# Where the first keys are loaded: one of four opening loads of an attention and feed-forward kernel moves from a hardware queue to the software queue

## The chip, the cores and the metric

The kernel runs on one core of a Trainium2 chip. The core has five engines that run their own instruction streams and meet through semaphores: TensorE (PE) multiplies matrices, VectorE (DVE) and ScalarE (ACT) work on tiles, GpSimd (POOL) does the same and also issues DMAs whose descriptors it writes in software, and SyncE (SP) issues DMAs. DMAs issued from SP and ACT go through hardware queues. In this kernel all DMAs that change the type on the way, from f32 in memory to bf16 in the core, are issued from POOL. All DMAs share the core's 16 DMA engines. The metric is the device time of one execution in microseconds, median over several runs.

## The reference

The inputs q, k and v have the shape 8 x 8 x 576 x 64 (batches, heads, tokens, width of a head), all f32. Each token attends to itself and the 63 tokens before it in its batch. The result, as 4608 rows of 512, goes through a gated feed-forward block of width 1536:

```python
scores = scale * np.matmul(q, k.transpose(0, 1, 3, 2))
rel = pos[:, None] - pos[None, :]
scores = np.where((rel >= 0) & (rel < 64), scores, -1e9)
attn = softmax(scores)                      # with max and sum along the last axis
x = (attn @ v).transpose(0, 2, 1, 3).reshape(4608, 512)
g = x @ w_gate
out = (g / (1 + exp(-g)) * (x @ w_val)) @ w_out
```

## The kernel before

The 4608 tokens are cut into 36 tiles of 128 and 9 blocks of 512. Of a tile the kernel needs q and k transposed (a head's width on the partitions), from which it makes scores, exponentials, and their product with v; the result is normalised and transposed to `xT`. Of a block it makes the gate and value products with the weights `Wg` and `Wv` (12 groups of 128 columns each, four matmuls a group), the activation, and the product with `Wo`. Matmuls of the feed-forward block are most of TensorE's time. The order of the work on each engine is written out by hand in `build`: `_Graph` keeps one list of operations, gives each engine its operations in that order, and derives the semaphore waits from the keys that an operation reads and writes.

This study is about the head of the program, the first four tiles (tokens 0 to 255 are the first pair, 256 to 511 the second), which must go through attention before the feed-forward matmuls of block 0 can start:

- `loads` puts out, in this order: `first_loads`; `init` (DVE memsets, and two selects on POOL that make the triangle `tri` and the identity `ident`); `init_mask` and `init_nmask` (DVE operations that make the masks from `tri`); some memsets; then POOL's queue: `load2(1)` (q and k of the second pair, tiles `ks` and `qs`, gated on the mask `nmask`), four loads of v (`va`), the first weights (`W(0, 2)`: Wg and Wv of column groups 0 and 1), a copy of v to shifted rows (`shift`), and more weights and shifts.
- `first_loads` (L830) loads q and k of the first pair, as f32, into a part of a buffer that is still free (`hT`). Each is split into the even and the odd heads, so there are four loads of 256 KB: k even on SP, k odd on ACT, then q even on SP and q odd on ACT. A partition holds eight tokens of one head, 2 KB in one piece.
- `first_cast` (L840) turns these rows to bf16, in the buffer `ost`: k even on DVE, k odd on ACT, q even on DVE, and q odd in two parts, five of eight tokens on DVE and three on ACT.
- `first_T` (L848) transposes on TensorE. For the first pair a transpose takes 128 columns (a token's even and odd head side by side), eight for each of k and q. For the second pair, whose rows hold the even heads first and then the odd ones, it takes 64 columns, sixteen for each.
- `first_ev` copies the transposed rows out of PSUM to `kT` and `qT`.
- `warm(5)` puts five dummy f32 matmuls on a tile of zeros ahead of everything on TensorE.

On TensorE the order of the head is: the dummies, k's transposes, q's transposes, four matmuls that put the mask bias into PSUM, scores of tile 0, the second pair's transposes between further bias matmuls and scores, the products with v, the transposes to `xT`, and from then on the gate and value matmuls of block 0 (L918).

Of the kernel before, what the change touches and what calls it, by code (L numbers as in the profile page):

```python
# [17 lines left out]
BF = dt.bfloat16  # L18
# [135 lines left out]
class _Kernel:  # L154
# [18 lines left out]
    def alloc(self):  # L173
        nc = self.nc

        def sb(name, n, dtype=BF):
            return nc.alloc_sbuf_tensor(name, [128, n], dtype)

        def ring(name, cnt, n, dtype=BF):
            return [sb("%s%d" % (name, i), n, dtype) for i in range(cnt)]  # L180

        self.ident = sb("ident", 128)
        self.tri = sb("tri", 128)
        self.mask = sb("mask", 3 * 128)
        self.nmask = sb("nmask", 3 * 128)
        self.kmask = sb("kmask", 128)
        self.Wg = sb("Wg", NK * DFF)[:, :].rearrange("p (c f) -> p c f", c=NK)
        self.Wv = sb("Wv", NK * DFF)[:, :].rearrange("p (c f) -> p c f", c=NK)
        self.Wo = sb("Wo", NF * DM)[:, :].rearrange("p (c m) -> p c m", c=NF)
        self.qn = ring("qn", self.NQ, DM)  # L190
        self.kn = ring("kn", self.NQ, DM)
        self.rows = {x: ring(x + "s", 2, 2 * DM) for x in "qk"}
        self.va = [t[:, :].rearrange("p (h d) -> p h d", h=H) for t in ring("va", self.NV, H * 80)]
        self.vs = [t[:, :].rearrange("p (h d) -> p h d", h=H) for t in ring("vs", 4, H * 80)]
        self.kT = sb("kT", 4 * self.NZ * 128)[:, :].rearrange("p (c t) -> p c t", c=4)
        self.qT = sb("qT", 4 * (self.ZQ * 128 + 64))[:, :].rearrange("p (c t) -> p c t", c=4)
        self.wz = sb("wz", 512)
        self.pt = [t[:, :].rearrange("p (h x) -> p h x", h=H) for t in ring("pt", self.NP, H * 128)]
        self.rc = ring("rc", 2, 8, F32)
        self.xb = ring("xb", 4, DM)  # L200
        xT = ring("xT", self.NX, NK * 512)
        self.xT = [t[:, :].rearrange("p (c t) -> p c t", c=NK) for t in xT]
        self.sig = ring("sig", self.NS, 512)
        self.uu = ring("uu", self.NS, 512)
        hT = ring("hT", self.NH, NF * 512)
        self.hT = [t[:, :].rearrange("p (f t) -> p f t", f=NF) for t in hT]
        self.ost = ring("ost", self.NO, DM, F32)
        self.first = {}
        for i, x in enumerate("kq"):
            f = hT[1][:, 2048 * i:2048 * i + 2048].bitcast(F32).rearrange("p (e j d) -> p e j d", e=2, j=8)  # L210
            c = self.ost[i][:, :].bitcast(BF).rearrange("p (j e d) -> p j e d", j=8, e=2)
            self.first[x] = (f, [("hT", 1, 4 * i + f, j) for f in range(4) for j in range(2)], c, [("ost", i), ("osth", i)])
        self.wup = sb("wup", 1, F32)
        self.psa = nc.alloc_psum_tensor("ps", [128, 4096], F32)
        self.ps = [self.psa[:, 512 * i:512 * i + 512] for i in range(8)]
        self.rot = {"f": ([0, 1, 2, 3], 0), "a": ([4, 5, 6, 7], 0)}
        self.n_s = 0
        self.lru = False
        self.held = set()
# [610 lines left out]
        return ev  # L830

    def first_loads(self):
        for x, src in (("k", self.k), ("q", self.q)):
            f, fkeys, _, _ = self.first[x]
            for e0, eng in ((0, "sp"), (1, "act")):
                a = src[0, e0::2, 0:256, :].rearrange("c (g j) d -> g c (j d)", j=8)
                d = f[:, e0].rearrange("p j d -> p (j d)")
                self.g.op(eng, lambda e, d=d, a=a: e.dma_start(d, a), reads=fkeys, writes=[("f", x, e0)], dma=True)

    def first_cast(self, x, parts):  # L840
        f, fkeys, c, ckeys = self.first[x]
# [4 lines left out]
    def first_T(self, x, st=0):  # L846
        c, ckeys = self.lines(1, x) if st else (self.first[x][2], self.first[x][3] + self.first[x, 0])
        bank, bk = self.bank("a")  # L848
        tb = bank.bitcast(BF).rearrange("p (j t) -> p j t", j=8)

        def pe(e):
            for j in range(8):
                if st:
                    for p in range(2):
                        r = e.transpose(tb[64 * p:64 * p + 64, j, :], c[:, j, p, :], self.ident[:, :])
                else:
                    r = e.transpose(tb[:, j, :], c[:, j, :, :], self.ident[:, :])
            return r

        self.g.op("pe", pe, reads=["ident"] + ckeys, writes=[bk])  # L860
        return bank, bk
# [195 lines left out]
    def build(self):  # L1057
# [1 line left out]
        self.loads()  # L1059
        self.banks("a", [4, 5, 6, 7, 0, 1, 2, 3, 4, 5, 0, 1, 2, 3, 4, 5, 6, 7, 0, 1, 2, 3, 4, 5, 6, 7, 6, 7])  # L1060
        self.lru = True
        self.warm(5)
        self.first_cast("k", ((0, 0, 8, "dve"), (1, 0, 8, "act")))
        self.first_cast("q", ((0, 0, 8, "dve"), (1, 0, 5, "dve"), (1, 5, 8, "act")))
        fk = self.first_T("k")
        self.first_ev("k", 0, "dve", fk)
        fq = self.first_T("q")
# [208 lines left out]
```

## Time and profile before

| what | value |
|---|---|
| median of 3 runs | 325.6 us (325.49 to 325.85) |
| profiled execution, its own time | 325.72 us |
| span of the profiled execution | 324.0 us |
| TensorE matmuls, busy | 314.4 us, 97% |
| VectorE, busy | 218.6 us, 67% |
| ScalarE, busy | 125.6 us, 39% |
| GpSimd, busy | 106.5 us, 33% |
| software DMA queue | 100032 packets, 18.36 MB |
| hardware DMA queues | 48336 packets, 20.72 MB |

Rows of the timeline give the start in microseconds from the span's start, the duration, the engine, the line and the operation with its output and inputs; in square brackets stands how long the engine was idle before and what ended that. Rows of the chain give start, duration and what held the chain. "SPq", "ACTq" and "POOLq" are the sequencers that issue DMAs. An issue row ends when the descriptors are written, not when the data has landed; the last number of a DMA row tells the time from issue to landing. The KB of a DMA are those that it writes.

### The profile page before, as it was taken

How to read it: one execution, taken by the hardware profiler on the slowest of the kernel's cores; microseconds unless marked ns; L12 is line 12 of the kernel's file. 1: busy time of each engine (PE TensorE's matmuls, PEld its weight loads, DVE VectorE, ACT ScalarE, POOL GpSimd, SP SyncE). 2: the span in 40 equal slices, each digit the busy share in tenths (PEclk: the TensorE clock that was granted, in tenths of full speed). 3: DMA queues.
4: the chain of work that ended last, by engine and by line, in shares of the span. 5: the costliest groups of instructions: out<-in, count | busy, mean ns of one | idle time of the engine just before them, and what ended most of it. 6: DMA issues, size and time to landing. Idle time of an engine off the chain costs nothing.

```text
span 324.0 us, 8018 instructions
## 1 busy us (share of the span) xinstructions
PE 314.4 (97%) x3411; PEld 169.3 (52%) x3446; DVE 218.6 (67%) x408; ACT 125.6 (39%) x226; POOL 106.5 (33%) x138
## 2 busy tenths in 40 slices
PE   7989999999999999999999999999999999999996
PEld 5655677777545454545454544545454544444444
DVE  6778985788576966766767585958586767555510
ACT  3825565643433442433333232424242422222311
POOL 6999711643626061507060607060402000000000
PEclk9999999999999999999999999999999999999999
DMA  7999999999999799959997998999677212000012
GB/s 189 177 197 187 201 184 176 104 169 142 166 155 152 124 109 137 165 103 133 129 120 118 146 139 83 148 133 159 73 110 96 69 34 65 34 32 32 34 65 97
DMA packets 148403, 39.59 MB, mean 122 GB/s; under 512 B 131344, under 2 KB 143376, under 8 KB 148368
## 3 DMA queue, kind: packets, MB, share of 16 engines
q0 software_dynamic: 100032, 18.36, 71.7%
q1 hardware_dynamic: 42864, 10.89, 23.5%
q10 hardware_dynamic: 5472, 9.83, 9.5%
q8 instruction: 27, 0.44, 0.6%
q14 instruction: 8, 0.07, 0.1%
HBM read 37.75 MB, written 9.44 MB: 146 GB/s over the span
## 4 chain that ended last, share of the span: by engine, by line
PE 91%; DMA 2%; POOL 2%; issue 1%; DVE 1%; ACT 1%; ACTq 0%
PE ps L918 56%; PE ps L962 29%; DMA Wv<-in_moe_w_val_dram 2%; PE ps L729 2%; PE ps L521 2%; POOL va L325 1%; PE ps L471 1%; PE ps L475 0%; ACT xT L255 0%; PE ps L385 0%; ACT sig L899 0%; POOL ks L335 0%; PE ps L552 0%; POOL qs L335 0%; POOL Wg L345 0%
## 5 line engine op out<-in xcount | busy, mean ns | idle before, releaser
L918 PE MATMUL ps<-xT,Wv 128*128 128x512 bf16 (+1 forms) x484 | 110.4, 351 | 1.6 <-DMA Wv<-in_moe_w_val_dram 0.9
L904 DVE SCALAR_TENSOR_TENSOR uu<-sig,ps 128x512 bf16<-128x512 bf16 x108 | 73.8, 683 | 56.2 <-ACT sig L899 55.9
L918 PE MATMUL ps<-xT,Wg 128*128 128x512 bf16 (+1 forms) x481 | 107.9, 351 | 2.3 <-issue 2.2
L899 ACT ACTIVATE sig<-ps 128x512 bf16<-128x512 f32 x108 | 64.9, 603 | 89.1 <-PE ps L918 89.1
L962 PE MATMUL ps<-Wo,hT 128*128 128x512 bf16 (+1 forms) x436 | 97.4, 373 | 0.5 <-DVE hT L906 0.2
L906 DVE SCALAR_TENSOR_TENSOR hT<-uu,ps 128x512 bf16<-128x512 bf16 x108 | 74.2, 687 | 4.7 <-PE ps L918 1.0
L918 PEld LDWEIGHTS ps<-xT,Wv 128*128 128x128 bf16 x496 | 48.4, 98 | 45.7 <-DMA Wv<-in_moe_w_val_dram 1.1
L918 PEld LDWEIGHTS ps<-xT,Wg 128*128 128x128 bf16 x496 | 46.8, 98 | 42.7 <-ACT xT L255 0.2
L962 PEld LDWEIGHTS ps<-Wo,hT 128*128 128x128 bf16 x444 | 43.3, 98 | 49.0
L325 POOL DMA_DIRECT2D kn<-in_k_dram x27 | 23.0, 855 | 112.0 <-PE ps L918 112.0
L325 POOL DMA_DIRECT2D va<-in_v_dram x40 | 34.2, 882 | 24.9 <-PE ps L918 24.9
L255 ACT ACTIVATE ost<-ps 128x512 f32<-128x512 f32 (+1 forms) x22 | 12.9, 588 | 53.2 <-PE ps L962 53.2
L531 ACT ACTIVATE pt<-ps 128x512 bf16<-128x512 f32 x36 | 18.6, 602 | 29.0 <-PE ps L521 29.0
L256 DVE COPY ost<-ps 128x512 f32<-128x512 f32 (+1 forms) x15 | 10.1, 673 | 29.2 <-PE ps L962 29.2
L325 POOL DMA_DIRECT2D qn<-in_q_dram x27 | 23.2, 865 | 0.0
L483 ACT ACTIVATE pt<-ps 128x512 bf16<-128x512 f32 x28 | 14.5, 602 | 13.8 <-PE ps L475 13.8
L764 DVE TENSOR_TENSOR xb<-ps,rc 128x512 bf16<-128x512 f32 (+2 forms) x39 | 18.8, 509 | 0.5
L729 PE MATMUL ps<-va,pt 64*64 64x65 bf16 x800 | 12.3, 192 | 0.0
L497 DVE TENSOR_TENSOR pt<-pt,kmask 128x1024 bf16<-128x1024 bf16 x18 | 11.5, 681 | 0.0
L729 PEld LDWEIGHTS ps<-va,pt 64*64 64x64 bf16 x800 | 10.4, 107 | 0.0
L497 DVE TENSOR_TENSOR pt<-pt,mask 128x1024 bf16<-128x1024 bf16 x14 | 9.3, 688 | 1.1 <-ACT pt L483 1.0
L760 DVE RECIPROCAL rc<-ps 128x8 f32<-128x8 f32 (+2 forms) x39 | 5.7, 173 | 6.3 <-PE ps L729 6.3
(76 smaller groups left out, 141.7 us busy)
## 6 DMA issues: line engine op xcount, KB each, us to landing
out_dram<-ost ACTq DMA_DIRECT2D x35, 256.0 KB, 3.3
va<-in_v_dram POOLq DMA_DIRECT2D x32, 128.0 KB, 5.3
kn<-in_k_dram POOLq DMA_DIRECT2D x21, 128.0 KB, 3.9
qn<-in_q_dram POOLq DMA_DIRECT2D x21, 128.0 KB, 4.7
Wg<-in_moe_w_gate_dram POOLq DMA_DIRECT2D x6, 256.0 KB, 7.2
Wv<-in_moe_w_val_dram POOLq DMA_DIRECT2D x6, 256.0 KB, 8.2
Wo<-in_moe_w_out_dram POOLq DMA_DIRECT2D x4, 384.0 KB, 13.6
ks<-in_k_dram POOLq DMA_DIRECT2D x3, 256.0 KB, 10.5
```

The costliest lines, as they stand in the source:

```text
L255: return self.g.op("act", lambda e: e.activation(d, a, ACTF.Copy), reads=reads, writes=writes, after=after)
L325: self.g.op("pool", lambda e, d=d, a=a: e.dma_start(d, a), writes=ks, dma=True, after=gate)
L483: g.op("act", lambda e, po=po, p=p: e.activation(po, sv[p], ACTF.Exp, scale=SCALE), reads=[bx[p][1]], writes=[pk[p]])
L497: self.g.op("dve", lambda e: e.tensor_tensor(pt, pt, m, ALU.mult), reads=pk + mk, writes=pk)
L531: g.op("act", lambda e, po=po, p=p: e.activation(po, sv[p], ACTF.Exp, scale=SCALE), reads=[bx[p][1]], writes=[pk[p]])
L729: x = e.matmul(o, ab[0], ab[1], start=first, stop=phase == 1, skip_group_check=True)
L764: g.op("dve", lambda e, av=av, hs=hs, w=w, rc=rc, xo=xo: e.tensor_tensor(xo[:, :, hs, :], av[:, :, :, 0:64], rc[:, :, hs].unsqueeze(3).to_ ...
L899: g.op("act", lambda e: e.activation(sig[:, 0:w], G[:, 0:w], ACTF.Tanh, scale=0.5), reads=[gk], writes=[("sig", i)])
L904: g.op("dve", lambda e: e.scalar_tensor_tensor(uu[:, 0:w], sig[:, 0:w], 1.0, G[:, 0:w], ALU.add, ALU.mult), reads=[("sig", i), gk], writes ...
L906: g.op("dve", lambda e: e.scalar_tensor_tensor(out, v3(uu), 0.5, v3(V), ALU.mult, ALU.mult), reads=[("uu", i), vk], writes=[("hT", ih, f, ...
L918: r = e.matmul(bank[:, a * n:a * n + n], W[:, kk, f * 128:f * 128 + 128], xT[:, kk, lo:hi], start=(kk == 0), stop=(kk == NK - 1))
L962: r = e.matmul(OB[:, 0:n], hT[:, f, 128 * u:128 * u + 128], self.Wo[:, f, lo:hi], start=(f == 0), stop=(f == NF - 1))
```

## The change

The load of k's odd heads leaves ACT's hardware queue. It is issued by POOL as the first operation of its queue, ahead of the two selects, and it casts on the way: bf16 rows go straight into the second half of the buffer that the casts write for k, whose layout is now "even heads, then odd heads". So k needs one cast (its even heads, DVE) and is transposed in sixteen pieces of 64 columns as the second pair is. ACT's hardware queue loads q odd first (its only load of the four), SP's loads k even and then q even. q odd is now cast by ACT in one piece, and q even, the last to be issued, in two parts on DVE and ACT. One of five dummy matmuls goes.

```diff
-            c = self.ost[i][:, :].bitcast(BF).rearrange("p (j e d) -> p j e d", j=8, e=2)
+            c = self.ost[i][:, :].bitcast(BF).rearrange("p (e j d) -> p j e d" if x == "k" else "p (j e d) -> p j e d", j=8, e=2)
...
     def first_loads(self):
-        for x, src in (("k", self.k), ("q", self.q)):
+        for x, e0, eng in (("k", 0, "sp"), ("q", 1, "act"), ("q", 0, "sp")):
             f, fkeys, _, _ = self.first[x]
-            for e0, eng in ((0, "sp"), (1, "act")):
-                a = src[0, e0::2, 0:256, :].rearrange("c (g j) d -> g c (j d)", j=8)
-                d = f[:, e0].rearrange("p j d -> p (j d)")
-                self.g.op(eng, lambda e, d=d, a=a: e.dma_start(d, a), reads=fkeys, writes=[("f", x, e0)], dma=True)
+            src = self.k if x == "k" else self.q
+            a = src[0, e0::2, 0:256, :].rearrange("c (g j) d -> g c (j d)", j=8)
+            d = f[:, e0].rearrange("p j d -> p (j d)")
+            self.g.op(eng, lambda e, d=d, a=a: e.dma_start(d, a), reads=fkeys, writes=[("f", x, e0)], dma=True)
+        a = self.k[0, 1::2, 0:256, :].rearrange("c (g j) d -> g c (j d)", j=8)
+        d = self.ost[0][:, 256:512].bitcast(BF)
+        self.g.op("pool", lambda e: e.dma_start(d, a), writes=[("fc", "k", 1, 0)], dma=True)
+        self.first["k", 0] = [("fc", "k", 1, 0)]
...
             for j in range(8):
-                if st:
+                if st or x == "k":
                     for p in range(2):
                         r = e.transpose(tb[64 * p:64 * p + 64, j, :], c[:, j, p, :], self.ident[:, :])
...
-        self.warm(5)
-        self.first_cast("k", ((0, 0, 8, "dve"), (1, 0, 8, "act")))
-        self.first_cast("q", ((0, 0, 8, "dve"), (1, 0, 5, "dve"), (1, 5, 8, "act")))
+        self.warm(4)
+        self.first_cast("k", ((0, 0, 8, "dve"),))
+        self.first_cast("q", ((1, 0, 8, "act"), (0, 0, 5, "dve"), (0, 5, 8, "act")))
```

## The prediction

> **What bounds the kernel now.** I read the page first (engine shares), then the chain of work that ended last, then the timeline, DMA and wait views of the first 20 us, because the diff ends there. TensorE is the bound over the span; the page and the chain's first pieces:
>
> ```profile
> span 324.0 us, 8018 instructions
> PE 314.4 (97%) x3411; PEld 169.3 (52%) x3446; DVE 218.6 (67%) x408; ACT 125.6 (39%) x226; POOL 106.5 (33%) x138
> ...
> 8.42 0.71 POOL Wg L345
> 9.12 8.06 DMA Wv<-in_moe_w_val_dram
> ...
> 17.22 2.79 PE ps L918 x24
> ```
>
> From 17.22 us on the chain is TensorE work. So an edit to the head is worth what it does to 17.22. Before that the chain does not run through the q and k work that the change touches: it runs through POOL's DMA issues and the landing of the first Wv block, at 9.12 + 8.06 = 17.18. The PE timeline says the same:
>
> ```profile
> 14.32 0.19 PE L644 MATMUL ps<-vs,pt 128*64 128x65 bf16 x1 [0.33 <-POOL vs L256]
> 15.02 1.05 PE L918 MATMUL ps<-xT,Wg 128*128 128x256 bf16 x8
> 15.90 0.39 PE L821 MATMUL ps<-ident,xb 128*128 128x128 bf16 x4
> 17.22 1.05 PE L918 MATMUL ps<-xT,Wv 128*128 128x256 bf16 x8 [0.94 <-DMA Wv<-in_moe_w_val_dram]
> ```
>
> PE is through with all attention work of the head at 15.90 + 0.39 = 16.29 and sits 0.93 us until Wv lands. Whatever q and k gain ahead of that is not seen; whatever they lose up to 0.93 us is hidden. So the question is what the change does to the landing of Wv. The DMA view from 0 to 40 us, 1 us a column:
>
> ```profile
> DMA  0059999999999999999999999999999999999999
> GB/s 0 0 98 336 408 281 193 194 162 151 154 159 196 196 196 201 195 195 196 198 195 205 191 199 193 197 195 185 160 174 192 200 218 192 200 199 196 198 196 198
> ```
>
> The DMA engines are full from 3 us on: first f32 rows at some 400 GB/s, then cast rows at 195 written, which is 390 read. Wv's landing is a place in one full stream. Issue and landing of its parts (timeline rows, then rows of the DMA view over the instant of each issue; last number: us to landing):
>
> ```profile
> 8.38 0.79 POOL L345 DMA_DIRECT2D Wg<-in_moe_w_gate_dram  x1
> 10.71 0.74 POOL L345 DMA_DIRECT2D Wg<-in_moe_w_gate_dram  x1
> 11.44 0.76 POOL L345 DMA_DIRECT2D Wv<-in_moe_w_val_dram  x1
> ...
> Wg<-in_moe_w_gate_dram POOLq DMA_DIRECT2D x1, 256.0 KB, 5.7
> ...
> Wg<-in_moe_w_gate_dram POOLq DMA_DIRECT2D x1, 256.0 KB, 7.2
> ...
> Wv<-in_moe_w_val_dram POOLq DMA_DIRECT2D x1, 256.0 KB, 7.8
> ...
> q8 instruction: 1, 0.02, 60.1%
> ```
>
> Landings: first Wg 8.38 + 5.7 = 14.1, first Wv 17.18, second Wg 10.71 + 7.2 = 17.9, second Wv 11.44 + 7.8 = 19.2. A block of 256 KB at 195 GB/s takes 1.34 us, and the last gap is 1.3; but the first Wv comes 3.1 after its Wg and only 0.7 ahead of the next block. It is late by 17.18 - (14.1 + 1.34) = some 1.7 us, by itself. The last row is of the stretch 15.1 to 15.2: one instruction fetch packet, 60.1% of 0.1 us on 16 engines = 0.96 us on one of them, just where this Wv should have ended. I infer that one engine's share of Wv stands behind that fetch; the rows show the coincidence, not the cause. The page "Runtime: NRT & Kernel Launch" of the Trainium skill (Instruction fetch mechanics) says that an engine's instructions come in blocks of 16 KiB on a DMA queue of its own and that crossing a block is mostly hidden; the 0.02 MB row agrees in size, and by "hidden" the lateness would have another cause.
>
> **The change, part by part.** The first loads and casts (issue rows, landing rows, DVE and ACT):
>
> ```profile
> 0.81 0.66 SPq L838 DMA_DIRECT2D hT<-in_k_dram  x1
> 0.83 0.65 ACTq L838 DMA_DIRECT2D hT<-in_k_dram  x1
> 1.50 0.80 ACTq L838 DMA_DIRECT2D hT<-in_q_dram  x1
> 1.53 0.58 SPq L838 DMA_DIRECT2D hT<-in_q_dram  x1
> ...
> hT<-in_k_dram SPq DMA_DIRECT2D x1, 256.0 KB, 3.5
> hT<-in_k_dram ACTq DMA_DIRECT2D x1, 256.0 KB, 4.1
> hT<-in_q_dram ACTq DMA_DIRECT2D x1, 256.0 KB, 4.8
> hT<-in_q_dram SPq DMA_DIRECT2D x1, 256.0 KB, 4.1
> ...
> 4.33 0.43 DVE L256 CAST ost<-hT 128x512 bf16<-128x512 f32 x1 [0.49 <-DMA hT<-in_k_dram]
> 4.99 0.63 ACT L255 ACTIVATE ost<-hT 128x512 bf16<-128x512 f32 x1 [1.16 <-DMA hT<-in_k_dram]
> ```
>
> 1. One hardware load goes. The four land at 4.3, 4.9, 5.6 and 6.3: 0.65 us each in the full stream. Three are left.
>
> 2. A software load of the same rows comes, 128 KB written, 256 KB read, so by 195 GB/s written 0.67 us of the same engines. The stream ahead of Wv grows by 0.02. Its start may use the time in which the stream isn't full yet: the column of 2 us moved 98 KB and that of 3 us 336, where 408 is full. Software bytes follow their issue by some 2 us (ks, issued at 3.32, shows in the column of 5), so they can fill at most the lack of the column of 3 us: 72 of 408, 0.18 us. I take 0.1 of gain, bounds 0 and 0.18.
>
> 3. When it lands: the first software load of now, ks, takes 4.3 us (row below), the second Wv 7.8; issued at 0.83 that is 5.1 at best and near that, since nothing stands ahead of it on its queue. k is then whole at some 5.1 to 5.5, against 4.99 + 0.63 = 5.62. q's even half is now the last hardware load; with the software rows between it comes at 6.1 to 6.4, where q's odd half came at 6.3. Its cast is split as before, 5 parts DVE and 3 ACT. ACT's cast of k odd (0.63) goes and one of q odd, of the same shape, takes its place; DVE loses nothing but moves one cast. So q's transposes stand where they stood, within 0.2 us.
>
> 4. POOL's queue. The load stands ahead of the two selects that make the triangle and the identity, then ks, qs, v and the weights:
>
> ```profile
> 1.16 0.29 POOL L270 TENSOR_SCALAR_AFFINE_SELECT tri<-tri 128x128 bf16<-128x128 bf16 x1 [0.63 <-DVE tri L259]
> 1.55 0.31 DVE L259 MEMSET va<- 128x128 bf16 x2
> 1.77 0.16 DVE L290 COPY mask<-tri 64x192 bf16<-64x192 bf16 x1
> 3.26 0.59 DVE L259 MEMSET vs<- 128x128 bf16 x4
> 3.32 0.84 POOL L335 DMA_DIRECT2D ks<-in_k_dram  x1 [1.46 <-DVE nmask L299]
> ...
> ks<-in_k_dram POOLq DMA_DIRECT2D x1, 256.0 KB, 4.3
> ```
>
> An issue costs POOL 0.74 to 0.84. From 0.83 it ends at 1.67; the select of tri ends at 1.96 instead of 1.45; the mask copies, at 1.77 until now because DVE was in its memsets until 1.86, start at about 2.1: 0.3 late. nmask, which gates ks, is 0.3 late, so every POOL issue is. DVE's own row holds: its memsets end at 3.26 + 0.59 + 0.3 = 4.15, ahead of k's landing at 4.3. For the stream the 0.3 us is nothing as long as other bytes fill it: ks's bytes began in the column of 5 us (281 between 408 and 193) while hardware rows ran to 6.3, and the first load's own 0.67 us come in between. The v loads and weights queue behind a full stream (5 to 8 us from issue to landing). I take 0; bounds 0 and 0.3.
>
> 5. POOL's shifts of v stand behind these issues and feed the PE row at 14.32 above:
>
> ```profile
> 10.15 0.61 POOL L256 COPY vs<-va 64x512 bf16<-64x512 bf16 x1 [0.24 <-DMA va<-in_v_dram]
> 12.24 1.93 POOL L256 COPY vs<-va 64x512 bf16<-64x512 bf16 x3
> ```
>
> 0.24 of the 0.3 us goes into that wait; the copies end some 0.1 late and PE's 16.29 becomes 16.4. Cover: the wait for Wv.
>
> 6. PE: one dummy less, and k's transposes in 16 pieces instead of 8:
>
> ```profile
> 1.41 4.10 PE L877 MATMUL ps<-wz 128*128 128x224 f32 x10 [1.41 <-DVE wz L259]
> 5.67 0.83 PE L857 MATMUL ps<-ident,ost 128*128 128x128 bf16 x8 [0.16 <-ACT ost L255]
> 6.94 0.61 PE L857 MATMUL ps<-ident,ost 128*128 128x128 bf16 x8 [0.44 <-DVE ost L256]
> 8.67 0.64 PE L855 MATMUL ps<-ident,ks 128*64 128x128 bf16 x16
> ```
>
> A dummy is two of the ten, 0.8 us, and ends the warm-up at 4.7. Sixteen half transposes took 0.64 later, against 0.83 or 0.61 for eight: 0.2 less to nothing more, in idle PE time ahead of q. Net twelve more instructions in PE's stream (a dummy is two loads and two matmuls, a transpose one of each), so fetches fall earlier in its program.
>
> **Sum.** Stream -0.1, POOL 0, PE 0 (under the wait of 0.93): 17.22 becomes 17.1. The profiled execution took 325.72 (span 324.0 and 1.7 around it), 0.12 above the median of 325.6. So 325.62 for such a run, and 325.5 against the median. 0.2%, or 0.65 us, is about what a measurement of this kernel can tell from no change.
>
> **Rivals.**
> Faster: the fetch, moved by the twelve instructions, no longer stands at the end of Wv. Wv then lands by 15.4 to 16.4, and PE's own 16.4 decides: 17.22 - 16.4 = 0.8 less, 324.8. For it: the whole 0.93 hangs on one packet's place. Against: the fetch waits in the same full stream, which hardly moves, and served one block earlier it would hold Wg instead, and with it PE.
>
> Slower: the first software issue is held while DVE runs its opening memsets. Place: POOL from 0.83. If it starts only at 1.86, tri ends near 3.0, nmask and every POOL issue are 1.3 late, ks's first bytes miss the end of the hardware rows by up to a microsecond and the full stream has a hole. It decides from about 0.3 us of hold; price up to 1.0, so 326.6. Against it: ks was issued beside memsets (3.26 and 3.32) in 0.84, with 0.74 later. The page "SBUF — State Buffer" of the Trainium skill (Who interferes with whom) says that POOL is shut out of a port pair which it shares with DVE for as long as a DVE operation in a two-port mode lasts, and so cannot write descriptors; by its example, 620 ns alone and 3100 under a copy, the issue would last some 4 us, an estimate from that page. The 0.84 row speaks for little of it.
>
> Clock: with less PE work before 5.7 us PE could go to its full rate later than now (0.83 for eight transposes at 5.67, 0.61 at 6.94). All that PE runs from 6.94 to the ks transposes at 8.67, at half its rate, costs at most the 1.73 that it spans; less 0.93 of cover that is 0.8 at most, and I take half of it: 325.9.
>
> Without effect: the software rows come last of all, at 0.83 + 5.7 = 6.5, and k's transposes push q's back by 0.64: hidden in 0.93, 325.6.
>
> **Chances.** Likeliest as summed 0.38 (own range 325.1 to 326.0); fetch elsewhere 0.32; issue held 0.19; clock 0.07, less than half of it above 0.65; no effect 0.04. Faster 0.32; within 0.2% 0.38 + 0.04 + 0.04 = 0.46; slower 0.19 + 0.03 = 0.22. The range goes from the whole wait gone, 325.5 - 0.93 = 324.6, to the held issue, 326.6.
>
> **What would show it.** Right: POOL's first DMA issue near 0.8 lasting 0.75 to 0.85, mask copies near 2.1, ks issued near 3.65, k's transposes at 5.1 to 5.5, PE waiting again 0.5 to 1 us for Wv at about 17.1, an instruction packet near 15. Wrong: the first L918 row on Wv at 16.4 with no wait (fetch), a first issue above 1.2 us or a column below 190 GB/s between 5 and 8 us (held), transposes of q at over 0.8 us (clock).

## The result and the profile after

The changed kernel takes 326.81 us (median of 7 runs, 326.19 to 327.54), the kernel before 325.49 (7 runs beside them, 325.05 to 325.85). The ratio is 1.0043 with a 95% interval of 1.0028 to 1.0057: slower by 0.43%, 1.3 us. The prediction, 325.5 with a range of 324.6 to 326.6, was wrong. The profiled execution has a span of 325.1 us, 1.1 more than before.

The opening rows of the timeline of the changed kernel (L841 is the new load):

```profile
0.81 0.65 SPq L838 DMA_DIRECT2D hT<-in_k_dram  x1
0.82 0.65 ACTq L838 DMA_DIRECT2D hT<-in_q_dram  x1
1.34 0.69 POOL L841 DMA_DIRECT2D ost<-in_k_dram  x1 [0.82 <-POOLq L1265]
1.52 0.58 SPq L838 DMA_DIRECT2D hT<-in_q_dram  x1
2.15 0.29 POOL L270 TENSOR_SCALAR_AFFINE_SELECT tri<-tri 128x128 bf16<-128x128 bf16 x1
2.47 0.28 DVE L290 COPY mask<-tri 64x192 bf16<-64x192 bf16 x1 [0.62 <-POOL tri L270]
4.13 0.72 POOL L335 DMA_DIRECT2D ks<-in_k_dram  x1 [1.44 <-DVE nmask L299]
```

The new issue lasts 0.69 us, but it begins at 1.34, not at 0.83. So the select of tri is at 2.15 (before 1.16), the first mask copy at 2.47 (1.77), ks at 4.13 (3.32): POOL's queue is 0.8 us late. What this does to the stream is seen in the DMA view from 0 to 16 us, 40 columns of 0.4 us. Before:

```profile
GB/s 0 0 0 0 0 72 92 205 318 399 405 410 405 328 174 200 189 187 189 200 176 151 147 152 156 155 155 154 151 167 193 200 192 200 195 196 193 236 187 181
DMA packets 6904, 2.92 MB, mean 183 GB/s; under 512 B 4300, under 2 KB 6391, under 8 KB 6903
```

After:

```profile
GB/s 0 0 0 0 0 56 148 328 251 271 305 213 310 341 156 26 143 187 200 184 202 205 148 131 128 139 144 151 147 156 161 170 178 191 192 198 197 191 234 187
DMA packets 6569, 2.63 MB, mean 164 GB/s; under 512 B 4286, under 2 KB 6184, under 8 KB 6568
```

The sixteenth column (6.0 to 6.4 us) holds 26 GB/s where before it held 200. The first loads are through at about 6.0 but for a last part, and the rows of ks, issued 0.8 later, are not there yet. By 16 us 0.29 MB less is written; 0.13 of that is the f32 that is now bf16, and the other 0.16 MB is 0.8 us of stream at 195 GB/s. Some 0.1 MB of it is missing in the three columns around the hole. The landings and TensorE's rows behind it (DMA view of the issue's instants, then the timeline):

```profile
hT<-in_k_dram SPq DMA_DIRECT2D x1, 256.0 KB, 3.6
hT<-in_q_dram ACTq DMA_DIRECT2D x1, 256.0 KB, 4.2
ost<-in_k_dram POOLq DMA_DIRECT2D x1, 128.0 KB, 4.8
...
6.25 0.64 PE L859 MATMUL ps<-ident,ost 128*64 128x128 bf16 x16 [1.60 <-DMA ost<-in_k_dram]
7.03 0.61 PE L861 MATMUL ps<-ident,ost 128*128 128x128 bf16 x8
...
11.42 0.61 POOL L256 COPY vs<-va 64x512 bf16<-64x512 bf16 x1 [0.83 <-DMA va<-in_v_dram]
13.49 1.93 POOL L256 COPY vs<-va 64x512 bf16<-64x512 bf16 x3
...
15.57 0.19 PE L644 MATMUL ps<-vs,pt 128*64 128x65 bf16 x1 [0.32 <-POOL vs L256]
...
17.28 1.04 PE L922 MATMUL ps<-xT,Wv 128*128 128x256 bf16 x8
```

POOL's shifts end 1.25 us later than before (13.49 against 12.24), TensorE's last product with v comes 1.25 later (15.57 against 14.32), and the wait of 0.94 for Wv is gone: PE arrives at Wv at 17.28, as before at 17.22. The loss of the profiled execution is not here. It is at the products with v of tiles 4 and 5, the third pair (L620), which read what POOL's next copies leave (`halves(4)` and `halves(5)`, four copies; the texts below call these two tiles chunks). Timeline rows of before:

```profile
31.52 3.31 POOL L256 COPY vs<-va 64x512 bf16<-64x512 bf16 x4
...
35.28 0.22 PE L620 MATMUL ps<-vs,pt 128*64 128x65 bf16 x1
```

And of the changed kernel:

```profile
32.79 3.42 POOL L256 COPY vs<-va 64x512 bf16<-64x512 bf16 x4
...
36.35 0.19 PE L620 MATMUL ps<-vs,pt 128*64 128x65 bf16 x1 [0.58 <-DVE uu L908]
```

The four copies end at 34.83 before and at 36.21 after. L620 does two tiles: the first starts in both kernels at 35.3, the second at 35.53 before, without a wait, and at 36.35 after. The row names DVE as what came last, but POOL's copies end 0.14 ahead of it, and two experiments show nearly the same distance, 0.15. From ks on POOL has one issue or copy after the other until these copies, but for its wait for v at about 10 us (0.24 before, 0.83 after). So what it is late behind that wait it is late here. The second tile had 0.55 us to spare (34.83 + 0.15 against 35.53); 1.38 late leaves 0.8 of loss, and TensorE's rows stand 0.8 later from there. Another 0.3 comes later in small steps.

### The profile page after: what moved, and what is told of

Read it like the earlier page. It is cut to its first block, busy times and chain, and to the rows that moved or that the text cites. A ratio compares the mean times of both kernels' runs of the same rounds, so it can differ in the third digit from the quotient of the medians.

```text
span 325.1 us, 8064 instructions
## 1 busy us (share of the span) xinstructions
PE 317.1 (98%) x3452; PEld 168.7 (52%) x3452; DVE 218.3 (67%) x407; ACT 125.8 (39%) x226; POOL 107.1 (33%) x139
## 4 chain that ended last, share of the span: by engine, by line
PE 92%; POOL 3%; DVE 1%; ACT 1%; issue 1%; POOLq 0%
PE ps L922 57%; PE ps L966 29%; PE ps L729 2%; PE ps L521 2%; POOL va L325 1%; PE ps L471 1%; POOL vs L256 1%; ACT pt L483 1%; PE ps L385 1%; POOL Wv L345 0%; POOL Wg L345 0%; PE ps L475 0%; DVE uu L908 0%; ACT xT L255 0%; PE ps L620 0%
## 5 line engine op out<-in xcount | busy, mean ns | idle before, releaser
L922 PE MATMUL ps<-xT,Wg 128*128 128x512 bf16 (+1 forms) x496 | 111.2, 352 | 0.1
L966 PE MATMUL ps<-Wo,hT 128*128 128x512 bf16 (+1 forms) x444 | 98.7, 373 | 0.0
```

The source lines that it names most:

```text
L922: r = e.matmul(bank[:, a * n:a * n + n], W[:, kk, f * 128:f * 128 + 128], xT[:, kk, lo:hi], start=(kk == 0), stop=(kk == NK - 1))
L966: r = e.matmul(OB[:, 0:n], hT[:, f, 128 * u:128 * u + 128], self.Wo[:, f, lo:hi], start=(f == 0), stop=(f == NF - 1))
```

## The experiments

Each time stands beside runs of the kernel before on the same chip (325.4 to 325.5 in all four groups). Each kernel ran twelve times unless another number is given; the text before each result says what was expected. The theories: POOL (its queue is late), Stream (the changed loads themselves cost), TensorE or clock (one dummy less, later full rate).

**The load behind the selects.** In the changed kernel, the software load moves to a function of its own that `loads` calls behind `init`:

```diff
         self.init()
+        self.first_soft()
         self.init_mask()
```

> The changed kernel with one thing undone: POOL issues the load of k's odd heads behind its two selects instead of ahead of them. Three theories. POOL: the change costs 1.3 us because its issue holds POOL's queue (selects, masks, ks and all later loads and copies) 0.8 us late, and POOL has no idle time in which to catch up before TensorE needs its copies at L620 (36 us). Stream: the software rows among the hardware rows slow the loads themselves. TensorE: the shorter warm-up, the sixteen half transposes or the instruction fetches that they move cost it. POOL expects the selects back near 1.2 and 1.6, ks issued at 3.3 to 3.6 and a time of 325.3 to 325.8 where the kernel before has 325.5. Stream and TensorE expect the time of the changed kernel, 326.8.

326.14 us, ratio 1.0019 (1.0009 to 1.0030): about half of the loss is left (0.76 of 1.3 us by the medians, 0.19 of 0.43% by the ratios). That lies outside POOL's range of 325.3 to 325.8, and it is not the 326.8 of the other two theories either. The selects are back at 1.16, ks at 3.31. In the profiled execution, one of the faster (325.76), POOL is late again further on:

```profile
10.47 0.61 POOL L256 COPY vs<-va 64x512 bf16<-64x512 bf16 x1 [0.65 <-DMA va<-in_v_dram]
...
16.39 1.05 PE L924 MATMUL ps<-xT,Wv 128*128 128x256 bf16 x8
...
31.95 3.38 POOL L256 COPY vs<-va 64x512 bf16<-64x512 bf16 x4
...
35.48 0.19 PE L620 MATMUL ps<-vs,pt 128*64 128x65 bf16 x1 [0.59 <-DVE uu L910]
```

TensorE met Wv at 16.39, 0.83 earlier than before, and gave it back at L620, 0.15 us behind the end of POOL's copies (35.33), nearly the distance of the changed kernel, while DVE's row is another. The copies end 0.5 later than before (34.83) though ks was on time. POOL waited 0.65 us for v, which was issued 0.1 earlier than before and landed 0.3 later. So here the lateness came in with v's landing and not from the head of POOL's queue; why v lands later the runs do not show.

**POOL held by a memset of 0.95 us, all else as before.**

```diff
+        busy = self.pt[5]
+        self.g.op("pool", lambda e: e.memset(busy, 0.0), writes=[("pt", 5, 0), ("pt", 5, 1)])
```

> The kernel before with one thing added: a memset on POOL of 128x1024 bf16 on a tile not used until later, ahead of the selects; no load is moved. POOL expects the selects and ks some 0.7 to 1.1 us late, a copy of v at L256 that ends 0.7 to 1.3 late near 36 us, a wait of TensorE at L620, and 326.2 to 327.0. Stream and TensorE expect 325.5, since the loads, the bytes and TensorE's program are those of before.

325.72 us, ratio 1.0011 (1.0002 to 1.0021); ks is 0.5 late. POOL's 326.2 to 327.0 missed: the delay was smaller than expected, and 0.5 us of it costs 0.3 by the medians.

**The copies of `halves` ahead of two loads, in the changed kernel.**

```diff
-        self.load(6, "v")
-        self.load(7, "v")
         self.halves(4, "pool")
         self.halves(5, "pool")
+        self.load(6, "v")
+        self.load(7, "v")
```

> The changed kernel with POOL's queue rearranged at 30 us: the four copies of v (halves 4 and 5) go ahead of the loads of v 6 and 7 instead of behind them, 1.8 us earlier in the queue. POOL expects that TensorE's wait of 0.6 us at L620 goes, and 326.0 to 326.3; if the loss at L620 is only where a loss made elsewhere shows, it comes back later and the time stays 326.8, which is also what Stream and TensorE expect.

326.67 us, ratio 1.0042 (1.0027 to 1.0058): no gain, against POOL's 326.0 to 326.3. The wait at L620 is gone (POOL's copies end at 35.2), but the loss is at the other gate:

```profile
18.32 0.94 PE L922 MATMUL ps<-xT,Wv 128*128 128x256 bf16 x7 [0.84 <-DMA Wv<-in_moe_w_val_dram]
```

So L620 alone is not the cause; in this execution the late stream showed at Wv. Of the 16 completion marks that the trace has for this Wv, 15 stand by 16.41 and the last at 18.28, with an instruction packet at 16.07. Before has the same picture (15.35, 17.18, packet at 15.15), the changed kernel not (16.57, 16.86), though a packet stands at 15.53 there too. That the fetch holds Wv is not shown.

**TensorE's part alone.** The kernel before with four dummies, k's new layout and its sixteen transposes.

```diff
-            c = self.ost[i][:, :].bitcast(BF).rearrange("p (j e d) -> p j e d", j=8, e=2)
+            c = self.ost[i][:, :].bitcast(BF).rearrange("p (e j d) -> p j e d" if x == "k" else "p (j e d) -> p j e d", j=8, e=2)
...
-                if st:
+                if st or x == "k":
...
-        self.warm(5)
+        self.warm(4)
```

> The kernel before with TensorE's part of the change alone: four dummies instead of five, k's layout with the even heads first and its transposes in sixteen pieces; loads, queues and casts as before. TensorE expects 326.5 or more. POOL and Stream expect 325.5. The idea of the prediction, that TensorE's wait for Wv hangs on an instruction fetch that falls at the end of its landing, expects the landing of Wv to move when twelve instructions more stand ahead of it, to 16.4 or less if the fetch no longer meets it, and the time then 0.5 to 0.9 below before.

325.63 us, ratio 1.0008 (0.9996 to 1.0019): TensorE's part alone is within what can be told from nothing. Its profiled execution bears on the prediction's idea of the fetch. The last mark of the first Wv stands at 14.89, 2.3 us earlier than in the profile of before, and nothing is won, because TensorE comes to it no earlier:

```profile
17.23 1.04 PE L918 MATMUL ps<-xT,Wv 128*128 128x256 bf16 x8
```

Its transposes of q took 1.01 us here where they took 0.61 before (the last section has such rows). So the wait of 0.94 for Wv is not in every execution, even with the loads of before.

**No wait for nmask.** The changed kernel, with POOL going on to ks at once:

```diff
-        self.load2(1, done)
+        self.load2(1)
```

> The changed kernel with one thing less: ks is issued without waiting for nmask, so POOL's issues follow its two selects at once. Before this run: 326.8 for the changed kernel, 325.4 for before. POOL theory (POOL's unbroken chain of issues and copies started 0.8 us late, and TensorE meets its end at L620): ks starts at 2.7 to 3.0 instead of 4.13, the hole in the stream at 6 us closes (column above 170 GB/s), POOL's copies for chunks 4 and 5 end by 35.0 instead of 36.2, time 325.0 to 325.7. Stream theory (three hardware loads and a software one of 128 KB leave a hole whatever POOL does, v lands late): column of 6 us stays near 100, va0 lands after 10.9, time above 326.2. TensorE theory (a dummy less, full clock later): 326.2 to 327, whatever POOL does.

326.03 us, ratio 1.0012 (0.9999 to 1.0026): with the changed loads all in place the loss is down to 0.6 of 1.3 us by the medians, 0.12 of 0.43% by the ratios. POOL's range of 325.0 to 325.7 was still missed. The rows show the early ks and, in the 0.4 us columns, no hole (146 and 182 where the changed kernel has 156 and 26):

```profile
2.40 0.29 POOL L274 TENSOR_SCALAR_AFFINE_SELECT ident<-ident 128x128 bf16<-128x128 bf16 x1
2.64 0.72 POOL L335 DMA_DIRECT2D ks<-in_k_dram  x1
...
GB/s 0 0 0 0 0 61 102 374 318 251 302 230 356 323 146 182 179 190 187 200 160 167 157 156 154 154 155 154 157 173 189 197 193 197 196 197 229 186 182 196
```

That speaks against the Stream theory, which said above 326.2 and a hole whatever POOL does. POOL's copies end at 34.7, in time, and L620 does not wait. The profiled execution (326.40) is 0.6 late already where TensorE meets Wv; its transposes and bias matmuls are the slow rows of the last section.

**The fifth dummy put back** (`self.warm(5)` in the changed kernel).

> The changed kernel with the fifth dummy put back. TensorE theory: the matmuls reach full rate by 6 us again in most executions, time 325.5 to 326.2, and a narrower spread than 326.2 to 327.5. POOL theory: POOL's rows stay as in the changed kernel (ks at 4.1, copies end at 36.2), time 326.4 to 327.0. Stream theory: as the POOL theory, no change.

326.41 us (325.81 to 326.50), ratio 1.0024 (1.0012 to 1.0036): lower than the changed kernel and with the narrower spread that the TensorE theory expected, but the intervals overlap, and its 325.5 to 326.2 missed; POOL's 326.4 to 327.0 holds at its edge. In its profiled execution, the fastest, ks is at 4.13, but POOL does not wait for v, and the copies end at 35.3 instead of the expected 36.2.

**The load behind the selects and the copies early.** The edits of the first and the third experiment together.

> The changed kernel with its software load behind the two selects, and the copies for chunks 4 and 5 ahead of the loads of v 6 and 7. With the load behind the selects alone: 326.1, TensorE met Wv at 16.38, 0.84 us earlier than before, and gave 0.59 back at L620. POOL theory: the wait at L620 goes (POOL has these copies done 1.4 us earlier, by 34.0), and the 0.84 stays: 324.6 to 325.2. Stream theory: the landing of Wv varies with the instruction fetch, 16.3 to 18.3, so between 324.7 and 326.5 with a wide spread. TensorE theory: the later clock costs up to 0.8 now that no other wait covers it: 325.6 to 326.4.

326.64 us (325.41 to 327.98), ratio 1.0030 (1.0013 to 1.0047). The POOL theory's 324.6 to 325.2 missed, and the ranges of the other two as well: with ks on time and no wait at L620 in the profile, 1.2 us are lost and no theory here explains it. The profiled execution was one of the two best (325.42, TensorE 0.35 us ahead of before at the end), so it does not show what makes the others slow.

**The copies early in the kernel before.** The third experiment's edit there.

> The kernel before with the copies for chunks 4 and 5 ahead of the loads of v 6 and 7, nothing else. POOL theory: before waits for Wv at 17.2 and POOL's copies end at 34.84, just in time, so nothing is won: 325.2 to 325.6, and no wait at L620. Stream theory: the loads of v 6 and 7 come 1.4 us later, nothing needs them before 60 us: 325.2 to 325.6. TensorE theory: the same. A time below 324.9 would say that L620 held the kernel before too in most executions.

325.26 us, ratio 0.9996 (0.9977 to 1.0015): nothing, as expected.

**No gate and five dummies.** The changed kernel with `self.load2(1)` and `self.warm(5)`.

> The changed kernel without the wait of ks for nmask, and with the fifth dummy. Alone the first edit gave 326.0 (from 326.8), the second 326.4. Two causes (POOL late by 0.8 and TensorE's full clock later in part of the executions), both undone: 325.2 to 325.6, with no execution above 326.2. POOL theory alone (the dummy does nothing): 325.8 to 326.3. Stream theory (the loads themselves cost): not below 325.8 either, with v landing late in the profile.

325.69 us (325.23 to 327.00), ratio 1.0014 (1.0001 to 1.0027), just outside every range given, with four executions above 326.2. The dummy adds nothing that can be told from the run without it.

**Load behind the selects, copies early, five dummies.**

> The changed kernel with the software load behind the selects, the copies for chunks 4 and 5 ahead of the loads of v 6 and 7, and the fifth dummy. Without the dummy: 326.6, from 325.4 to 328.0, though its profiled execution had TensorE 0.35 us ahead of before to the end. If the late clock made that spread, it is gone: 324.8 to 325.4, below before, none above 326. If the transfers made it (the later loads of v, the fetches), it stays: 326 to 327 with the same spread. POOL theory alone says 324.8 to 325.4 too, without saying why the run without the dummy missed it.

326.44 us (325.04 to 327.08), ratio 1.0023 (1.0008 to 1.0037): the two groups stayed (six executions up to 326.2, six from 326.7), against the clock theory and the POOL theory, and as expected if the transfers make the spread.

**What holds the first software issue.** The changed kernel with two memsets more on DVE:

```diff
         self.zero(self.tri[:, :], ["tri"], 1.0)
+        for i in (4, 5):
+            self.zero(self.pt[i], [("pt", i, 0), ("pt", i, 1)])
         self.zero(self.wz[:, :], ["wz"])
```

> The changed kernel with two further memsets of 128x1024 on DVE right behind the one of tri, so that DVE writes from 0.9 to some 2.2 us without a pause. Only POOL's rows of the first 4 us are read. If DVE's memsets hold the first software issue (the rival of the prediction), it starts at the end of them, 2.1 to 2.4 instead of 1.34, or lasts over 1.2 instead of 0.69. If it is a start of POOL's own, it stays at 1.34 with 0.69.

```profile
1.13 1.03 DVE L259 MEMSET pt<- 128x512 uint32 x2
1.34 0.69 POOL L843 DMA_DIRECT2D ost<-in_k_dram  x1 [0.81 <-POOLq L1267]
```

This kernel ran once, for these rows (327.6 us). The issue stands at 1.34 with 0.69, as without them. DVE's memsets do not hold it. The experiment with the memset on POOL shows that POOL itself is ready earlier:

```profile
0.81 0.95 POOL L1000 MEMSET pt<- 128x1024 bf16 x1 [0.29 <-POOLq L1263]
```

So a software DMA as POOL's first operation starts 0.53 us later than a memset there. Behind the selects POOL was idle 0.25 ahead of it (issued at 2.12), and in the kernel without the gate ks, the second such issue, followed a select with no gap.

**POOL late by the change's 0.8, all else as before.** Two memsets, so that ks is issued at 4.07:

```diff
+        a, b = self.pt[5], self.pt[4]
+        self.g.op("pool", lambda e: e.memset(a, 0.0), writes=[("pt", 5, 0), ("pt", 5, 1)])
+        self.g.op("pool", lambda e: e.memset(b[:, 0:2, :], 0.0), writes=[("pt", 4, 0), ("pt", 4, 1)])
```

> The kernel before with POOL held by two memsets ahead of its selects, so that ks is issued at 4.1 as in the changed kernel, 0.8 late, and all loads stay as before. One memset (0.5 late) gave 325.7 against 325.4. POOL theory: POOL's copies for chunks 4 and 5 end at 35.9 to 36.3 and the time is 325.9 to 326.5. Stream theory (the changed kernel lost by its loads, POOL's 0.8 is inside Wv's wait of 0.93): 325.4 to 325.8. TensorE theory: 325.4 to 325.7.

326.43 us (nine runs, 325.63 to 328.09), ratio 1.0029 (1.0015 to 1.0042), in POOL's range and above those of the other two: POOL's lateness alone, with before's loads and dummies, gives most of the loss (1.0 of 1.3 us by the medians, two thirds by the ratios). The profiled execution was the slowest of them. Its rows of 3 us (PE busy, granted clock, DMA share, GB/s) and of the timeline:

```profile
12.00:15.00 3.00, 1.40 (x56) 1.00 1.67 185
15.00:18.00 3.00, 2.71 (x46) 0.65 1.46 194
18.00:21.00 3.00, 3.00 (x25) 0.78 1.34 174
...
13.45 0.22 PE L644 MATMUL ps<-vs,pt 128*64 128x65 bf16 x1 [1.22 <-DVE vs L256]
...
17.05 1.92 PE L918 MATMUL ps<-xT,Wg 128*128 128x256 bf16 x8
```

A wait of 1.22 us for the shifted rows of v left TensorE over half idle between 12 and 15; then its granted clock fell to half from 15.9 to 19.3, and eight matmuls on Wg took 1.92 instead of 1.05. In this execution late POOL cost more than its lateness.

The mean clocks of all runs show how often this happens. Half the clock for 3.4 of 326 us makes a mean clock of 0.995, which this execution has. A mean of 0.995 or less stands in 11 of 45 executions of the five kernels in which ks is issued at about 4.1 (3 of 7 of the changed kernel, its three slowest), and in 8 of 257 of all others that ran in these experiments. The other four executions of the changed kernel have a median of 326.5, so some 1.0 us of its loss is there without it. Not every such kernel has it (none of twelve with five dummies).

**Six dummies in the changed kernel** (`self.warm(6)`).

> The changed kernel with six dummies instead of four, which fill TensorE up to about 6.3 us, when its k is there at 6.25. Four gave 326.8 (326.2 to 327.5), five 326.4 (325.8 to 326.5). Clock theory (an idle stretch of TensorE ahead of k's transposes leaves it at half rate for a further 3.4 us in part of the executions): 325.9 to 326.3, with no execution above 326.6, and eight of q's transposes in 0.61 to 0.75. POOL theory alone: 326.4 to 326.8, as before. Stream theory: the same.

326.80 us (five runs), ratio 1.0046 (1.0033 to 1.0059): no gain. With 326.81, 326.41 and 326.80 for four, five and six dummies no effect of the dummy is seen. The profiled execution, its fastest (326.07), has the pair of rows at L620 again:

```profile
32.44 3.29 POOL L256 COPY vs<-va 64x512 bf16<-64x512 bf16 x4
...
35.88 0.19 PE L620 MATMUL ps<-vs,pt 128*64 128x65 bf16 x1 [0.27 <-POOL vs L256]
```

Copies end at 35.73, L620 0.15 behind; here the row names POOL.

**Load behind the selects, copies early, six dummies.**

> The changed kernel with the software load behind the selects, the copies for chunks 4 and 5 ahead of the loads of v 6 and 7, and six dummies. With five: 326.4, from 325.0 to 327.1 in two groups, TensorE idle from 5.3 to 6.4. Clock theory: the sixth dummy fills that idle stretch, the upper group (above 326.1) goes, 324.9 to 325.4. Stream theory (the upper group comes from transfers): the two groups stay, 326.0 to 326.7.

325.70 us (324.77 to 327.22), ratio 1.0015 (1.0000 to 1.0030): between the two ranges. It is lower than with five, but two of 12 runs are still at 327.2, and the intervals overlap.

**No gate, copies early, six dummies.** The changed loads all kept:

> The changed kernel without the wait of ks for nmask, the copies for chunks 4 and 5 ahead of the loads of v 6 and 7, and six dummies. With five and without the earlier copies: 325.7 (325.2 to 327.0). Here k is there at 5.4, so the sixth dummy delays k's transposes to 6.0 to 6.3, inside the time that q needs anyway. POOL and clock theory together: 324.9 to 325.4, none above 326. If the changed loads cost something of their own: 325.5 to 326.

325.50 us, ratio 1.0004 (0.9993 to 1.0015): the same as before, with the changed loads kept. It is 0.1 above the range of POOL and clock together and at the edge of the other, and two executions are above 326. Which of the three edits the gain over the run without the gate is due to, the runs do not separate.

**No gate and copies early in the kernel before.**

> The kernel before without the wait of ks for nmask, and with the copies for chunks 4 and 5 ahead of the loads of v 6 and 7. The second edit alone gave 325.3 against 325.5. POOL theory: POOL starts 0.7 us earlier than before, Wv lands up to 0.7 earlier (16.5) unless the fetch holds it: 324.8 to 325.3. Stream theory (the stream is full either way, Wv's place in it is set by the bytes): 325.2 to 325.6. A rival to both: software rows that start earlier take the stream from the hardware loads, k and q come later: 325.5 to 326.2.

325.45 us, ratio 1.0001 (0.9988 to 1.0015): nothing won, though ks is issued at 2.11 instead of 3.32:

```profile
ks<-in_k_dram POOLq DMA_DIRECT2D x1, 256.0 KB, 7.0
...
9.16 0.64 PE L855 MATMUL ps<-ident,ks 128*64 128x128 bf16 x16 [0.59 <-DMA ks<-in_k_dram]
```

It lands at 9.1, where it landed at 7.6 when issued 1.2 later. That it shares the stream with the hardware loads would explain it, but no run isolates this. Early is of no use here; late makes a hole.

No version was found that beats the kernel before.

## Why the prediction was wrong, point by point

In short, the step that failed is the fourth, POOL's queue. It was taken to be 0.3 us late and hidden. It is 0.8 us late at ks and 1.3 us late at the copies of v, and the wait for Wv that was to hide it covers only the first of the two places where TensorE meets POOL's work.

1. Right: three hardware loads, landing at 0.81 + 3.6 = 4.4, 5.0 and some 6.3.
2. Wrong in sign: a gain of 0.1 us of stream was taken; 0.8 us of stream is missing by 16 us. The cause is step 4, not the load's own bytes: with ks early the hole is closed (2.78 MB by 16 us, where before's 2.92 less the 0.13 of the shorter rows is 2.79).
3. k's odd rows land at 1.34 + 4.8 = 6.1, not 5.1 to 5.5: 0.5 by the later start, 0.5 by a longer way (in the profiles of the copies early and of no gate it landed at 5.6 and 5.5, so the longer way is of that execution). q's transposes are at 7.03 against 6.94, within the 0.2 given, so this costs nothing.
4. This step failed, and decided: it took POOL's queue as 0.3 us late and the cost as nothing, and ks was 0.81 late. "From 0.83 it ends at 1.67" had the duration right (0.69) and the start wrong (1.34). 0.53 of start and 0.69 of issue, with 0.12 until the select, less the 0.35 in which POOL had waited for tri anyway, are the 0.99 of the select; 0.8 of it reaches ks. "I take 0; bounds 0 and 0.3" for the stream then fell too: the bytes that were to fill the time were through at 6.0, and ks's came after. It is shown that this lateness is enough for most of the loss (the two memsets: +1.0 us), and that with ks early and all loads kept half of the loss or more goes (no gate: 1.3 down to 0.6 us). It is not shown that lateness at the head of the queue is all: with the load behind the selects ks is on time, and those four kernels still lose 0.3 to 1.2 us.
5. Failed as a consequence: the wait of 0.24 ahead of the shift did not take up the lateness but grew to 0.83, as v landed later still (11.36 against 10.10; 14 of its 16 completion marks stand by 10.60, and with five dummies, ks as late, the last stood at 10.42, so this part is of the execution). The cover of 0.93 was used up entirely. That it was there is a matter of the execution too: in the profiles of TensorE's part alone, of the one memset and of the copies early in the kernel before, all with the loads of before, TensorE does not wait for Wv. The prediction took one profiled execution for the kernel. What the step did not look for is a second gate behind the first: behind the wait for v POOL works without a pause up to the copies for L620, and there only 0.55 us were to spare.
6. Right: sixteen half transposes in 0.64, in idle time; the dummy shows no effect that these runs can tell.

Of the rivals, "Slower" is what happened: a first issue held by over 0.3 us, a hole in the stream. Its mechanism for the hold was wrong, as the longer memsets on DVE show: the issue lasted 0.69 beside 1.03 us of memsets. The page "SBUF — State Buffer" of the Trainium skill (Who interferes with whom) names copies, casts and `tensor_scalar` as the operations of DVE that can take the shared pair in a two-port mode; memsets are not among them. So the rule was used there for operations that it does not name, and the run does not speak against the page. The price of this rival, up to 1.0, left out L620 and came 0.2 us short of 326.8. "Faster" happened in part: Wv, issued 0.68 later, landed by 16.9, earlier than 17.2, but neither TensorE nor POOL was there to use it. "Clock" did not happen in the profiled execution (q's transposes took 0.61), but its half rate did in other profiles, with the loads of before too (1.01 in that of TensorE's part alone).

What stays open: how the loss divides between Wv, L620 and a fallen clock changes from execution to execution, and one profile shows one of them. Why the versions with the load behind the selects lose time with ks on time, some with two groups of times over 1 us apart, is not settled; neither dummies nor the early copies removed it. In all four of their profiles, and in that of no gate, the first v lands 0.2 to 0.3 us later than in the profile of before though it is issued earlier. With the loads of before and ks on time it lands between 9.67 and 10.86 us in three profiles, so a cost of the changed loads themselves is neither shown nor excluded. Why a first software issue starts late isn't shown either.

## What to carry to other kernels

Cost an operation put at the head of a queue by its start as well as its duration, and follow the delayed engine until it next has idle time: here POOL had one short wait in 30 us, which gave nothing back, so 0.8 us in the masks came up as a wait at 36 us. A cover of 0.9 us at the next gate hides only what that gate sees; look for the same engine's next consumer and how much it has to spare. An engine that feeds a full stream must not be late where one kind of traffic ends and the next begins, while being early there bought nothing in the kernel before. And a wait read from one profiled execution can be absent from the next: look at several before it is taken as cover.

## What the runs showed of the hardware

- A software DMA as POOL's first operation started at 1.34 us, where a memset started at 0.81; its 0.69 us did not change under 1.03 us of DVE memsets.
- A DMA issued earlier can land later: ks issued at 2.11 landed at 9.1, issued at 3.32 at 7.6.
- TensorE's rate in the head differs between executions: eight transposes of q took 0.61 us in the profiles of before and after, and 1.01 here, in the kernel without the gate (the first three rows of this stretch), with a granted clock of 1.00 shown in both; the bias matmuls took 1.91 against 1.03. The trace's first record of a full clock stands at 6.16 us before, at 4.39 after and at 10.85 here, so the 1.00 shown ahead of it is no reading:

```profile
5.66 1.06 PE L859 MATMUL ps<-ident,ost 128*64 128x128 bf16 x16 [0.90 <-DMA ost<-in_k_dram]
6.83 1.01 PE L861 MATMUL ps<-ident,ost 128*128 128x128 bf16 x8
7.64 1.91 PE L427 MATMUL ps<-nmask,ident 128*128 128x512 bf16 x4
```

- In the execution with the two memsets the granted clock fell to half for some 3.4 us after TensorE had been idle for 1.6 of 3 us (0.65 and 0.78 in the rows above). In the profile of the changed kernel it was idle for 1.06 of the same 3 us, and the clock stayed at 1.00.
